# Attention with mixed heads and an expert layer: eight score tiles in a ring inside a larger tile, and a late store in two parts

## The chip, the core and the metric
The kernel runs on one core of one Trainium2 chip. The metric is the time of one execution on the device in microseconds (us). Before the change the median of three runs is 1441.89 us.

## The reference
```python
scores = scale * np.matmul(q, k.transpose(0, 1, 3, 2))       # 8 batches, 12 heads, 448 x 448
scores = np.einsum('bhij,hg->bgij', scores, w_pre)           # heads mixed
scores = scores - np.max(scores, axis=-1, keepdims=True)
attn = np.exp(scores)
attn = attn / (np.sum(attn, axis=-1, keepdims=True) + 1e-09)
attn = np.einsum('bhij,hg->bgij', attn, w_post)              # heads mixed again
x = np.matmul(attn, v)                                       # to (8*448, 12*64)
out = (((x @ w1) * (x @ w2)) @ w3) @ w_out                   # the expert layer
```
All of it is float32; the expert weights are 64-bit words in HBM that the kernel turns into floats itself.

## The kernel before
The main loop in `run` goes over steps n. A block is 10 rows of scores (queries) with all 12 heads; there are 45 blocks in a batch, and one step stands for one block. Work goes in pairs m of blocks, two steps for each.

Scores pass through HBM to change their layout. `qk` computes 128 rows of scores for two heads into two PSUM banks (psq, L174), ACT copies them into an SBUF tile `st` (L179, L180), and one DMA stores the tile to `raw_d` (L188; L185 for the last 64 rows of a pair). `fetch` reads a pair of blocks back (L202) with heads and rows on the partitions, two DMAs into a tile `r` of which there are two. `mix` multiplies it with the first head matrix (psm, L220), `largest` takes row maxima on DVE (L227), `exp` runs on ACT (L235), `scale` makes the second head matrix divided by the sums (DVE L244, L245, POOL L247), `post` multiplies with it (pso, L260), and `put` copies the result to a tile `mt` (ACT L274). `mt` holds 150 columns of queries; there are two buffers of it. `av` multiplies an `mt` block with v (psa, L301).

Beside that, `converting` turns the words of w3, w_out and later w1 and w2 into floats: a DMA into a tile cs (L103, five of them), a square on ACT (cm, L110), four instructions on DVE (cx, L121 to L124), then a split into two parts (ACT L129, POOL L130). `folding` multiplies w3 with w_out (psf, L360).

All order is written out by hand: each engine runs its instructions as the loop emits them, and nothing is rescheduled. SP issues every DMA in that order, and a DMA waits on SP for the landing of what it reads and for the semaphore that it takes; eight semaphores (DMAHW0 to DMAHW7) are taken in turn.

Score tiles come from two pools with two tiles each: `kp`, and for odd pairs of heads of batch 0 `qp`, which is closed at step 16. Before the loop, the first 128 rows of batch 0 are computed for all 12 heads into one tile `sz`. It takes the first of the two `mt` buffers, of which it uses 12 x 448 of 7200 columns. Its rows 0 to 47 are stored at once, in six DMAs; rows 48 to 127 in one DMA, `held`, behind the first two fetches and one DMA of weight words. Block pair 2 (rows 40 to 59) reads from both. The second `mt` block is first written by the `put` of step 17. In the loop, steps 0 to 11 compute the other rows of batch 0, steps 12 to 14 its last 64 rows, and from step 11 on the scores of batch 1 are added, about three units in four steps.

Of the kernel before, what the change touches and what calls it, by code (L numbers as in the profile page):

```python
# [6 lines left out]
F32 = mybir.dt.float32  # L7
# [8 lines left out]
B, H, S, D = 8, 12, 448, 64  # L16
DM, FF = 768, 1024
HP = H // 2
# [3 lines left out]
QT, NJ = 128, 4  # L22
# [5 lines left out]
PP = 64  # L28
JB = S // PP
SETS = NB * B // 2  # L30
FIRST = 48
# [2 lines left out]
LATE = 2 * NB + GB + 2  # L34
PAIRS = ((0, 0), (0, 1), (1, 0))
N_UP, NS = 20, 50
DEEP = 5
ONE = 2


# [10 lines left out]
class Kernel:  # L51
# [44 lines left out]
    def ask_words(self, depth):  # L96

        while len(self.asked) < depth and self.sources:
            src, n = self.sources.pop(0), self.n_words
            s = self.cs.tile([128, CW, 2], I32, tag="s", name=f"cs{n}", bufs=DEEP)  # L100
            a, k = src.shape[1], src.shape[2] // 2
# [30 lines left out]
    def converting(self, jobs, late=False):  # L132
# [5 lines left out]
        for n in range(len(jobs) + 1):  # L138
            self.ask_words(min(3 + self.n_made // 2, DEEP))
            yield  # L140
# [19 lines left out]
    def parts(self, b, p, c):  # L160
# [2 lines left out]
            return [(self.kqs[0, p], j * PP + S * (j > 1), QT) for p, j in pairs]  # L163
        return [(self.kqs[b, p], j * PP, S) for p, j in pairs]

    def qk(self, b, p, c, banks):


        nc = self.nc
        ps = [self.bank(i, f"psq{b}_{p}_{c}_{s}")[:, :S] for s, i in enumerate(banks)]  # L170
        for z, (t, q, k) in enumerate(self.parts(b, p, c)):
            for s in range(2):
                rows = slice(s * D, (s + 1) * D)
                nc.tensor.matmul(ps[s][z * PP:(z + 1) * PP], t[rows, q:q + PP], t[rows, k:k + S], start=True, stop=True)  # L174
        if b == c == 0:
            st = self.sz[:, 2 * p:2 * p + 2]
        else:
            st = (self.qp if b == 0 and p % 2 else self.kp).tile([128, 2, S], F32, tag="st", name=f"st{b}_{p}_{c}", bufs=2)
        nc.scalar.copy(st[:, 0], ps[0])  # L179
        (nc.vector.tensor_copy if b == c == 0 else nc.scalar.copy)(st[:, 1], ps[1])  # L180
        raw = self.raw_d[b]
        if c == 3:
            def store():
                for z in range(2):
                    nc.sync.dma_start(raw[3 * QT:, 2 * (p + z) - 2:2 * (p + z)], st[z * PP:(z + 1) * PP])  # L185
            return store
        n = QT if b or c else FIRST
        return lambda: nc.sync.dma_start(raw[c * QT:c * QT + n, 2 * p:2 * p + 2], st[:n])  # L188
# [280 lines left out]
    def sums(self, w, f, k):  # L469
# [8 lines left out]
        def split(m, i):  # L478
            s = self.cs.tile([128, CW, 2], I32, tag="s", name=f"s{w}_{f}_{m}", bufs=DEEP)
            s = s.rearrange("p n b -> p (n b)").bitcast(F32)  # L480
            dst, x = self.s_d[w][m][f].rearrange("p (t n) -> p t n", t=2), y[:, i]
            hi, lo = s[:, :n], s[:, n:2 * n] if w < 2 else x
            nc.scalar.copy(hi.bitcast(F32R), x)
            nc.gpsimd.tensor_tensor(lo.bitcast(F32R), x, hi, op=ALU.subtract)
            if w < 2:
                self.later.append(lambda: nc.sync.dma_start(self.s_d[w][m][f], s))
            else:
                self.later.append(lambda: nc.sync.dma_start(dst[:, 0], hi))
                self.later.append(lambda: nc.sync.dma_start(dst[:, 1], lo))
# [251 lines left out]
    def run(self):  # L741
        nc, tc = self.nc, self.tc
# [29 lines left out]
            self.kqs[0, p] = self.qp.tile([128, 2 * S], F32, tag="kq", name=f"kqz{p}")  # L772
            nc.sync.dma_start(self.kqs[0, p][:, :QT + S], self.kq0[p][:, :QT + S])
        self.sz = self.mp.tile([QT, NJ, H, GB * IB], F32, tag="mt", name="sz")
        self.sz = self.sz.rearrange("p j g i -> p (j g i)")[:, :H * S].rearrange("p (h j) -> p h j", h=H)
        w = self.kp.tile([128, 2, S], F32, tag="st", name="wpre_s", bufs=2)[:, 0, :PP]
        self.wsc = cp.tile([128, PP], F32, name="wsc")
        nc.sync.dma_start(w, self.wpre)
# [2 lines left out]
        for p in self.pso:  # L781
            for s in range(2):
                at = (2 * NJ - 2 + s) * HK
# [11 lines left out]
        held = []  # L795
# [6 lines left out]
        next(fold_pieces)  # L802
        for f in held:
            f()
        held = lambda: nc.sync.dma_start(self.raw_d[0][FIRST:QT], self.sz[FIRST:])

# [67 lines left out]
        others(1)  # L876
        for m in range(LF // 2):
            self.fetch(m)
        next(fold_pieces)
        next(fold_pieces)  # L880
        held()
        next(fold_pieces)
        next(fold_pieces)
        self.mix(0)
# [4 lines left out]
        for n in range(N + 6):  # L889
# [45 lines left out]
            p, pieces = self.n_made - 1 if fold_pieces else 2 * KF + 3 * KF, None  # L935
            if avs.get(n):
                pass
            elif fold_pieces:
                f = (self.n_made - 1 - 2 * KF) // 3
# [112 lines left out]
```

## Time and profile before
| | us |
|---|---|
| median of three runs | 1441.89 |
| lowest, highest run | 1441.69, 1447.07 |
| the profiled execution | 1437.83 |
| its span, first to last instruction | 1436.1 |

| engine | busy us | share |
|---|---|---|
| PE (matmuls) | 1382.4 | 96% |
| ACT | 832.4 | 58% |
| DVE | 741.1 | 52% |
| POOL | 620.3 | 43% |

The profile is of one execution on the chip. Each engine's instructions have a start and a length there, and idle time before an instruction is put down to what ended it. A DMA shows twice: its issue on SP, and its landing, when the last of its 16 engines has told its semaphore. [...] The DMA share is the mean busy share of the 16 DMA engines; it can pass 1, since packets of one engine overlap.

### The profile page before, as it was taken

Reading aid. Unit: us, or ns where it says so; the run is one execution under the profiler, and the core shown is the slowest. Engines: PE = TensorE matmul, PEld = TensorE weight load, DVE = VectorE, ACT = ScalarE, POOL = GpSimd, SP = SyncE. Lnnn points to the kernel's source line nnn. Section 1 sums busy time; section 2 is a strip of 40 time slices with the busy share of each in tenths; the row PEclk is TensorE's granted clock in tenths of the full one; section 3 lists DMA queues with packets and bytes.
Section 4 is the critical chain, followed back from the end, with each engine's and each line's share of the span. In section 5 each row is a group of like instructions: output and inputs, shape, how many; then the busy total and the mean of one; then the engine's idle time right before and its main releaser. Section 6 shows DMA issues by size and latency. Waiting matters only on the chain.

```text
span 1436.1 us, 45775 instructions
## 1 busy us (share of the span) xinstructions
PE 1382.4 (96%) x18684; PEld 1055.2 (73%) x18684; DVE 741.1 (52%) x1497; ACT 832.4 (58%) x1952; POOL 620.3 (43%) x754
## 2 busy tenths in 40 slices
PE   5889999999999999999999999999999999999998
PEld 2457786776677667776777777777777777899988
DVE  6867566767544544432444436334444446345563
ACT  4867666777766666665656556556555445422231
POOL 2433233434433544532345336334335446446693
PEclk7989999999999999999999999999999999999999
DMA  8998789999999999999989979799879757698775
GB/s 294 366 326 279 236 270 322 320 312 317 324 286 348 355 356 330 362 346 349 287 275 290 320 259 280 249 323 354 288 229 281 241 177 223 195 337 270 231 232 171
DMA packets 203761, 416.87 MB, mean 290 GB/s; under 512 B 20528, under 2 KB 120112, under 8 KB 203472
## 3 DMA queue, kind: packets, MB, share of 16 engines
q1 hardware_dynamic: 203552, 413.94, 87.6%
q8 instruction: 149, 2.44, 0.7%
q14 instruction: 60, 0.49, 0.1%
HBM read 279.77 MB, written 134.09 MB: 288 GB/s over the span
## 4 chain that ended last, share of the span: by engine, by line
PE 82%; DMA 8%; DVE 4%; ACT 2%; issue 1%; POOL 1%; SPq 0%; DVEq 0%; POOLq 0%; ACTq 0%
PE e L702 21%; PE psa L301 11%; PE pso L260 10%; PE psm L220 9%; PE psq L174 7%; PE eg L522 5%; PE psf L360 4%; PE eo L553 4%; PE e2o L702 4%; PE e1o L702 4%; PE e3o L702 4%; DMA wu<-w_d 3%; DMA r<-raw_d 2%; DMA raw_d<-st 2%; ACT e L235 1%
## 5 line engine op out<-in xcount | busy, mean ns | idle before, releaser
L247 POOL TENSOR_SCALAR w<-wpo,ri 128x60 f32<-128x60 f32 x360 | 180.7, 518 | 485.1 <-DVE ri L245 465.3
L227 DVE TENSOR_REDUCE mn<-psm 128x1 f32<-128x448 f32 x360 | 207.7, 618 | 321.6 <-PE psm L220 321.3
L274 ACT COPY mt<-pso 128x480 f32<-128x480 f32 x352 | 197.9, 621 | 185.8 <-PE pso L260 185.6
L702 PE MATMUL e<-eh,wu 128*128 128x448 f32 x1008 | 296.8, 371 | 6.4 <-DVE c L656 3.2
L235 ACT ACTIVATE e<-psm,mn 128x448 f32<-128x448 f32 x360 | 226.8, 643 | 7.9 <-DVE mn L227 7.9
L702 PEld LDWEIGHTS e<-eh,wu 128*128 128x128 f32 x1008 | 187.5, 188 | 52.2 <-issue 26.8
L260 PEld LDWEIGHTS pso<-w,e 60*64 60x64 f32 x10080 | 175.2, 135 | 51.0 <-issue 42.5
L220 PE MATMUL psm<-r,wsc 60*64 60x448 f32 (+1 forms) x1440 | 191.2, 550 | 19.1 <-DVE cx L124 8.3
L260 PE MATMUL pso<-w,e 60*64 60x60 f32 x10080 | 199.1, 224 | 0.4 <-ACT mt L274 0.3
L702 PE MATMUL e<-el,wu 128*128 128x448 f32 x504 | 186.9, 371 | 0.0
L301 PE MATMUL psa<-mt,v 128*64 128x150 f32 (+1 forms) x2304 | 156.9, 292 | 4.1 <-ACT st L179 4.1
L301 PEld LDWEIGHTS psa<-mt,v 128*64 128x64 f32 x2304 | 143.6, 137 | 20.1 <-ACT st L179 6.7
L174 PE MATMUL psq<-kq 64*64 64x448 f32 x1176 | 154.6, 542 | 2.4 <-ACT st L179 2.4
L656 DVE TENSOR_TENSOR c<-c,e 128x448 f32<-128x448 f32 x168 | 101.7, 618 | 87.7 <-PE e L702 82.9
L179 ACT COPY st<-psq 128x448 f32<-128x448 f32 x162 | 86.4, 533 | 73.7 <-ACT mt L274 34.1
L522 PE MATMUL eg<-xh,wu 128*128 128x448 f32 x384 | 119.2, 381 | 6.3 <-DMA wu<-w_d 6.3
L641 POOL TENSOR_TENSOR el<-x,eh 128x448 fp32r<-128x448 f32 x90 | 103.7, 1170 | 32.8 <-ACT eh L640 29.9
L702 PEld LDWEIGHTS e<-el,wu 128*128 128x128 f32 x504 | 94.6, 188 | 22.5 <-issue 14.1
L174 PEld LDWEIGHTS psq<-kq 64*64 64x64 f32 x1176 | 60.8, 135 | 56.4 <-issue 28.8
L522 PEld LDWEIGHTS eg<-xh,wu 128*128 128x128 f32 x384 | 71.9, 190 | 38.7 <-issue 24.0
L244 DVE TENSOR_SCALAR sa<-sm 128x2 f32<-128x2 f32 x180 | 34.9, 194 | 113.6 <-ACT e L235 113.1
L180 ACT COPY st<-psq 128x448 f32<-128x448 f32 x162 | 87.6, 541 | 0.0
(99 smaller groups left out, 2010.1 us busy)
## 6 DMA issues: line engine op xcount, KB each, us to landing
r<-raw_d SPq DMA_DIRECT2D x344, 210.0 KB, 5.1
raw_d<-st SPq DMA_DIRECT2D x138, 448.0 KB, 6.1
wu<-w_d SPq DMA_DIRECT2D x104, 384.0 KB, 6.7
wu<-s_d SPq DMA_DIRECT2D x96, 384.0 KB, 4.8
wu<-w_d SPq DMA_DIRECT2D x51, 512.0 KB, 5.5
kq<-kq SPq DMA_DIRECT2D x42, 448.0 KB, 7.0
wu<-s_d SPq DMA_DIRECT2D x36, 512.0 KB, 4.9
x<-x_d SPq DMA_DIRECT2D x72, 224.0 KB, 5.7
```

The lines of the kernel that those rows point to most:

```text
L174: nc.tensor.matmul(ps[s][z * PP:(z + 1) * PP], t[rows, q:q + PP], t[rows, k:k + S], start=True, stop=True)
L220: nc.tensor.matmul(ps[s][c * PP:(c + 1) * PP, :S], self.wsc[k], r[k, c], start=True, stop=True)
L227: self.nc.vector.tensor_reduce(mn[:, s:s + 1], self.psm[m][s][:, :S], axis=AX.X, op=ALU.min)
L235: nc.scalar.activation(e, p[:, :S], AF.Exp, bias=mn[:, s:s + 1], scale=-1.0, accum_out=sm[:, s:s + 1])
L247: nc.gpsimd.tensor_scalar_mul(w2[:, s], self.wpo, ri[:, s:s + 1])
L260: nc.tensor.matmul(self.pso[c][z * PP:(z + 1) * PP, at:at + HK], e[k, j * PP:(j + 1) * PP], w2s[k, s], start=True, stop=True)
L274: self.nc.scalar.copy(dst.rearrange("p j g (s i) -> p j s g i", s=2), src)
L301: nc.tensor.matmul(self.psa[rows, g % 3, :W], v[:, j, rows], mt[:, j, 2 * g + s, :W], start=(j == 0), stop=(j == NJ - 1))
L522: nc.tensor.matmul(p, u[:, k % (K1 // 2), x], xs[y][:, k], start=(k == 0 and t == 0), stop=(k == K1 - 1 and t == 2))
L641: nc.gpsimd.tensor_tensor(lo, x, hi.bitcast(F32), op=ALU.subtract)
L656: nc.vector.tensor_tensor(a[out], a[to[0]], p, op=ALU.add)
L702: nc.tensor.matmul(p, w[:, k, x], ops[m, k][y], start=(k == 0 and t == 0), stop=(k == nk - 1 and t == 2))
```

## The change
From the first score tile of step 0 up to step 14, `next_st` hands out eighths of the buffer in which `sz` lies: eight places of 2 x 448 columns in turn, the first two behind the end of `sz`, then its six, then again from the start. From step 15 on tiles come from `kp`, two of them. The late store of rows 48 to 127 becomes two: 16 rows ahead of the next DMA of weight words, and 64 rows where the whole store stood.

```diff
-DEEP = 5
+DEEP, RING = 5, 14
...
+    def next_st(self, name):
+        if self.step > RING:
+            return self.kp.tile([128, 2, S], F32, tag="st", name=name, bufs=2)
+        self.n_st += 1
+        at = (self.n_st + HP - 1) % 8 * 2 * S
+        return self.sz_all[:, at:at + 2 * S].rearrange("p (h j) -> p h j", h=2)
...
-            st = (self.qp if b == 0 and p % 2 else self.kp).tile([128, 2, S], F32, tag="st", name=f"st{b}_{p}_{c}", bufs=2)
+            st = self.next_st(f"st{b}_{p}_{c}")
...
-        self.sz = self.sz.rearrange("p j g i -> p (j g i)")[:, :H * S].rearrange("p (h j) -> p h j", h=H)
+        self.sz_all, self.n_st = self.sz.rearrange("p j g i -> p (j g i)"), 0
+        self.sz = self.sz_all[:, :H * S].rearrange("p (h j) -> p h j", h=H)
...
-        held = lambda: nc.sync.dma_start(self.raw_d[0][FIRST:QT], self.sz[FIRST:])
+        rest = [lambda k=k: nc.sync.dma_start(self.raw_d[0][k], self.sz[k]) for k in (slice(FIRST, PP), slice(PP, QT))]
...
         for m in range(LF // 2):
             self.fetch(m)
+        rest[0]()
         next(fold_pieces)
         next(fold_pieces)
-        held()
+        rest[1]()
```

On SP, ahead of the loop, before (r are the fetches of pairs 0 and 1, cs the weight words, sz the tile of the first scores; the brackets name the semaphores that a DMA waits for):
```order
20 L202 DMA r_219<-raw_d 60x2x448 [waits DMAHW5_49,DMAHW4_49,DMAHW7_49,DMAHW3_49,DMAHW0_49]
21 L202 DMA r_219<-raw_d 60x2x448
22 L202 DMA r_222<-raw_d 60x2x448
23 L202 DMA r_222<-raw_d 60x2x448 [waits DMAHW6_49]
24 L103 DMA cs_225<-wo 128x768
25 L805 DMA raw_d<-sz 80x5376
26 L103 DMA cs_238<-wo 128x768 [waits DMAHW1_49]
```
The same place in the changed kernel:
```order
20 L209 DMA r_219<-raw_d 60x2x448 [waits DMAHW5_49,DMAHW4_49,DMAHW7_49,DMAHW3_49,DMAHW0_49]
21 L209 DMA r_219<-raw_d 60x2x448
22 L209 DMA r_222<-raw_d 60x2x448
23 L209 DMA r_222<-raw_d 60x2x448 [waits DMAHW6_49]
24 L813 DMA raw_d<-sz 16x5376
25 L103 DMA cs_226<-wo 128x768
26 L813 DMA raw_d<-sz 64x5376 [waits DMAHW1_49]
```
The 80 rows at place 25 are now 16 rows at place 24 and 64 at place 26; each DMA behind them stands one place later and takes the next semaphore.

On ACT, steps 15 to 17, before (st_1_0, st_1_1 and st_1_2 are score tiles of batch 1, mt_1 is the second mt block):
```order
112 L179 COPY st_1_0_1078<-psq_1_0_0_1072 128x448 [waits DMAHW3_49,PE_49]
...
118 L179 COPY st_1_1_1114<-psq_1_1_0_1108 128x448 [waits DMAHW1_49,PE_49]
...
122 L274 COPY mt_0_414<-pso_141 128x4x2x12x5 [waits PE_49]
123 L274 COPY mt_1_1165<-pso_142 128x4x2x12x5 [waits PE_49]
124 L179 COPY st_1_2_1180<-psq_1_2_0_1174 128x448 [waits DMAHW1_49,PE_49]
125 L180 COPY st_1_2_1180<-psq_1_2_1_1175 128x448 [waits PE_49]
```
The same rows in the changed kernel:
```order
112 L186 COPY st_1_0_1061<-psq_1_0_0_1055 128x448 [waits PE_49]
...
118 L186 COPY st_1_1_1097<-psq_1_1_0_1091 128x448 [waits PE_49]
...
122 L281 COPY mt_0_412<-pso_141 128x4x2x12x5 [waits PE_49]
123 L281 COPY mt_1_1148<-pso_142 128x4x2x12x5 [waits DMAHW4_49,DMAHW3_49,DMAHW5_49,DMAHW2_49,DMAHW6_49,DMAHW1_49,DMAHW7_49,DMAHW0_49,PE_49]
124 L186 COPY st_1_2_1163<-psq_1_2_0_1157 128x448 [waits DMAHW2_49,PE_49]
125 L187 COPY st_1_2_1163<-psq_1_2_1_1158 128x448 [waits PE_49]
```
No instruction moved on ACT. The copies of steps 15 and 16 wait for no DMA any more, the first write of the second mt block waits for eight, and the copy of step 17 waits for the store of step 15's tile, as before.

## Rows read from the trace of the kernel before
**Rows 1.** The page, part 1: busy us, share of the span, instructions.
```profile
PE 1382.4 (96%) x18684; PEld 1055.2 (73%) x18684; DVE 741.1 (52%) x1497; ACT 832.4 (58%) x1952; POOL 620.3 (43%) x754
```
**Rows 2.** Stretches (us): length, busy per engine, granted clock, DMA share, GB/s.
```profile
24.00:28.00 4.00, 3.78 (x16) 1.32 (x16) 1.36 (x4) 2.04 (x7) 1.79 (x3) 0.50 0.89 325
28.00:32.00 4.00, 3.47 (x15) 1.46 (x13) 3.72 (x7) 3.08 (x8) 1.00 (x1) 0.50 0.99 266
32.00:62.00 30.00, 25.55 (x410) 13.70 (x413) 28.23 (x57) 26.31 (x64) 13.25 (x18) 0.91 1.02 365
62.00:96.00 34.00, 25.42 (x294) 13.38 (x286) 23.54 (x44) 21.67 (x52) 11.53 (x14) 0.80 1.03 367
...
110.00:300.00 190.00, 185.80 (x2781) 139.91 (x2770) 130.03 (x272) 133.92 (x322) 64.74 (x91) 1.00 0.90 292
```
**Rows 3.** Timeline, ACT: start, us, instruction, idle before it and what ended that.
```profile
64.47 0.53 ACT L179 COPY st<-psq 128x448 f32<-128x448 f32 x1 [0.62 <-DMA raw_d<-st]
...
70.45 0.53 ACT L179 COPY st<-psq 128x448 f32<-128x448 f32 x1 [2.90 <-PE psm L220]
...
74.11 0.53 ACT L179 COPY st<-psq 128x448 f32<-128x448 f32 x1 [2.69 <-DMA raw_d<-st]
...
78.42 0.53 ACT L179 COPY st<-psq 128x448 f32<-128x448 f32 x1 [1.48 <-DMA raw_d<-st]
...
95.72 0.53 ACT L179 COPY st<-psq 128x448 f32<-128x448 f32 x1 [4.05 <-DMA raw_d<-st]
```
**Rows 4.** DMA from 62 to 96 us: issues, KB each, median us to landing.
```profile
DMA packets 6527, 12.48 MB, mean 367 GB/s; under 512 B 602, under 2 KB 4068, under 8 KB 6524
...
raw_d<-st SPq DMA_DIRECT2D x8, 448.0 KB, 7.6
r<-raw_d SPq DMA_DIRECT2D x9, 210.0 KB, 7.4
```
**Rows 5.** Timeline, SP: start and length of DMA issues.
```profile
26.99 0.81 SPq L202 DMA_DIRECT2D r<-raw_d  x2
...
77.41 1.40 SPq L202 DMA_DIRECT2D r<-raw_d  x2
...
84.20 1.10 SPq L185 DMA_DIRECT2D raw_d<-st  x2
```
**Rows 6.** Timeline, the other engines.
```profile
23.00 0.56 ACT L110 ACTIVATE cm<-cs 128x384 f32<-128x384 f32 x1 [4.47 <-DMA cs<-wo]
...
28.10 0.36 DVE L121 TENSOR_SCALAR cx<-cs 128x384 int32<-128x384 int32 x1 [2.60 <-DMA cs<-wo]
...
32.42 0.53 ACT L179 COPY st<-psq 128x448 f32<-128x448 f32 x1
...
88.22 0.59 PE L220 MATMUL psm<-r,wsc 60*64 60x448 f32 x1
...
90.58 3.59 PE L360 MATMUL psf<-fo,fw 128*128 128x384 f32 x19
...
96.31 3.28 PE L301 MATMUL psa<-mt,v 128*64 128x150 f32 x48 [2.13 <-ACT st L179]
```
**Rows 7.** Chain that ended last: start, us, what (a DMA from issue to landing).
```profile
17.18 0.42 SPq L805
...
17.65 10.36 DMA cs<-wo
...
87.56 8.09 DMA raw_d<-st
```
**Rows 8.** Waits of SP, 10 to 110 us: in total, times, longest.
```profile
SPq L202 <- DMA raw_d<-sz: 5.5, 3, 4.5
```
**Rows 9.** Three shorter stretches, columns as in rows 2.
```profile
92.12:95.54 3.42, 2.05 (x12) 1.73 (x10) 2.72 (x6) 0.00 (x0) 0.18 (x1) 1.00 1.02 379
518.79:522.20 3.41, 0.63 (x4) 0.34 (x3) 1.90 (x5) 3.04 (x8) 0.05 (x1) 1.00 1.02 324
522.20:525.61 3.41, 3.41 (x10) 2.87 (x11) 1.50 (x3) 0.00 (x0) 2.71 (x3) 0.50 1.03 408
```

## The prediction
> **What bounds the kernel now.** I read the page first: TensorE (PE) is busy for 96% of the span, ACT and DVE for little more than half [rows 1]. Such a share hides stages, so the second view was the table by stretches [rows 2]. From 110 us on PE is busy 185.80 of 190 us: what comes before counts only by when that stage begins. The change touches steps 0 to 17, which lie before 97 us. Two other limits rule there. From 32 to 62 us VectorE (DVE) is busy 28.23 of 30 us; it turns the 64-bit weight words into floats. From 62 to 96 us PE is busy 25.42 of 34, DVE 23.54, ACT 21.67, and the DMA share is 1.03 at 367 GB/s.
>
> The third view, the timeline of that stretch, shows what the engines wait for [rows 3]: ACT's copies of scores into an st tile stand still for 0.62, 2.90, 2.69, 1.48 and 4.05 us. Four are put down to the store that last read the tile. The second names PE's L220; but that copy needs only its own two score banks and its tile, so it was a store there too. A reader may take these 11.74 us for a lack of tiles. The fourth view says what is behind them [rows 4]: 12.48 MB in 35 transfers (the counts of that answer's nine rows), 357 KB each. SP's instructions show eight DMA semaphores in rotation, so eight transfers can be under way, and eight of 357 KB at 367 GB/s take 7.8 us. A 448 KB store takes 7.6 us from issue to landing and an r fetch 7.4. So the queue is full, and a landing is set by the bytes ahead of it, not by when its data was ready.
>
> **The change, part by part.** Matmuls, conversions, copies and their order on PE, ACT, DVE and POOL stay. SP gets one DMA more; bytes and the order of the others are the same.
>
> *The ring.* Up to step 14 a copy waits for the store eight tiles back, where it waited for one two to four back. The copies of rows 3 start 3.7 us apart or more; at half of that, eight tiles are still 15 us, twice what a store needs. So the waits of 0.62, 2.90, 2.69 and 1.48 us go, 7.69 in all. What is late next? What PE then asks for is itself a landing from the full queue. The r fetches issued from 77.41 on, the second within 1.4 us [rows 5], land at 7.4 us each by about 85.8; their mix ran at 88.22 [rows 6], so it comes 2.4 us sooner and no more. Then come step 17's scores. From step 15 the two old st tiles serve again: the copy of step 17 takes the tile of step 15, whose store was issued at 87.56 and landed 8.09 us later, at 95.65 [rows 7]. It stands behind the same bytes as before, so its landing does not move. That copy started at 95.72 [rows 3], and behind it PE's attention product (psa) at 96.31 [rows 6]; from there PE is the limit. The 7.69 us are given back as a longer wait before this copy. Value taken: 0; bounds -7.69 and 0.
>
> *The new wait.* The second block of mt lies in the ring's buffer, so its first write waits for all the ring's stores, on all eight semaphores. It stands on ACT just ahead of the step-17 copy; queued behind it are that copy, a cast, a square and the next exponentials, and PE's psa waits for the copy. The last ring stores were issued from 84.20 to 85.30 [rows 5]; even at 7.6 us they land by 92.9, 2.7 us under the copy's own release at 95.65. Cost 0; were that cover gone, whatever they land later than the copy's tile.
>
> *The late store.* Before, 80 rows (1680 KB) went in one transfer at 17.18 [rows 7]. The fetch of the third pair of blocks reads rows 48 to 59 out of it and was issued only at 26.99 [rows 5]; SP, which issues in order, stood 4.5 us for the landing [rows 8]. Now 16 rows go first and the fetch waits for them alone, so SP gets on some 4 us sooner. But the queue was hardly empty meanwhile: its share was 0.89 from 24 to 28 us and 0.99 from 28 to 32, at 325 and 266 GB/s [rows 2]. At the 365 GB/s of the next stretch these eight us would have given 4 x 40/365 + 4 x 99/365 = 1.5 us; if the rates come from the small rows of r and kqz, nothing. Against it stands one more issue on SP, 0.42 us like the old one's [rows 7]. Bounds -1.5 and +0.4; I take -0.5, nearest to the idle share (4 x 0.11 = 0.44). It would carry through to the landing at 95.65, since the queue stays full in between.
>
> The first words of the output weights now come behind 16 rows (336 KB), 0.9 us at 367 GB/s. ACT had stood 4.47 us for them until 23.00 [rows 6], so this moves to 23.9. The words behind the store land where they did, at 28.01 [rows 7], and DVE had idled 2.60 us before those [rows 6]: cost 0, and up to 0.9 if that slack is used up.
>
> The words behind the whole store landed 1.0 us after SP was released by it (28.01 against 26.99), 384 KB at about the queue's rate: transfers follow one another closely. [...]
>
> *PE's clock.* PE's last work ahead of psa, 19 psf matmuls at 90.58 to 94.17 [rows 6], would end about 2.4 us sooner, and PE would stand over 4 us for psa, where it stood 2.1. [...] At 0.50 from 95.8 to 99.0, 1.6 us of PE's work is lost, where PE is the limit. Bounds 0 (clock kept) and 3.3 (low for 6.6 us); I take 1.6.
>
> **The sum:** ring 0, new wait 0, late store -0.5, first words 0, clock +1.6: +1.1 us. On the profiled execution's 1437.83 us (span 1436.1 and 1.7 around it) that is 1438.9. The median of the runs was 1441.89, 4.06 above that execution, so the forecast is 1443.0.
>
> **Rivals.**
> *The tiles were the limit: faster.* If stores landed sooner once ACT runs ahead, the 7.69 us would be PE's: 1441.9 - 7.7 = 1434.2. For it: ACT's idle time names the stores. Against it: a share of 1.03 over 34 us leaves nothing to send sooner. It decides at one place: the store issued at 87.56 must land by about 88. [...]
> *The clock falls and comes back late: slower.* PE stands before psa, and the clock is at 0.50 for two stretches like that of rows 9, from 95.8 to 102.4: +3.3. If besides the queue gains nothing and the first words cost their 0.9, it is +4.2: 1446.1. [...] For it: from 24 to 32 us the clock stayed at 0.50 though PE was busy 7.25 of 8 us [rows 2]. Against it: after 522.20, with PE busy throughout, it was back after 3.41 us [rows 9].
> *The ring doesn't do what it says.* Its third copy writes into the old tile, so it waits for both parts of the late store. The store was through by 26.99, that copy ran at 32.42 [rows 6], 5.4 us later; were the second part that much later, all of the ring would stand behind it. Price 0 as the rows are: 1441.9.
>
> **How the numbers follow.** Forecast 0.70 (own range 1440.4, which is -1.5 with the clock kept, to 1444.8, which is +1.6 with late words and the issue), tiles 0.13, clock slower 0.12, ring idle 0.05. Half a per cent, 7.2 us, is about what a measurement of this kernel can tell from no change. Faster means under 1434.7: half of the first rival, 0.06. Slower means over 1449.1, past every priced case: 0.03. The same has the rest, 0.91. The range runs from 1436.5 (two thirds of the tiles' gain) to 1446.5.
>
> **What would show it.** Right: ACT's waits for stores between 64 and 85 us gone; its wait before the step-17 copy, or before the mt write ahead of it, grown to 8 us or more; psa within 1.5 us of 96.31; the DMA share still near 1.03 up to 96 us; the third pair's fetch issued at about 22.5; a stretch at 0.50 close behind 95.5. Wrong: psa several us sooner, or a DMA share clearly under 1 before it.

## The result and the profile after

The changed kernel has a median of 1446.51 us (1442.57 to 1451.02, 15 runs); the kernel before, timed beside it, 1441.75 (1439.82 to 1447.07, 15 runs). The ratio is 1.0030, 95% interval 1.0016 to 1.0043: 2.3 to 6.2 us slower. That is under half a per cent, but no longer zero. 1443.0 was forecast; the median lies at the upper edge of the forecast's range (1446.5) and outside the narrower one that it gave itself (1440.4 to 1444.8).

The page, part 1, for the changed kernel (busy us, share, instructions) answers to [rows 1]; its span is 1448.0 us. PE's busy time rose by 3.3 us, while the two profiled spans differ by 11.9, so most of the difference is waiting:
```profile
PE 1385.7 (96%) x18684; PEld 1057.3 (73%) x18684; DVE 742.4 (51%) x1497; ACT 832.0 (57%) x1952; POOL 619.7 (43%) x754
```
Stretches of the changed kernel, with the columns of [rows 2]:
```profile
24.00:28.00 4.00, 3.46 (x16) 1.12 (x16) 1.65 (x5) 2.37 (x7) 1.79 (x3) 0.66 0.86 190
28.00:32.00 4.00, 1.25 (x6) 0.68 (x3) 0.18 (x1) 0.19 (x1) 0.00 (x0) 0.91 0.87 263
32.00:62.00 30.00, 23.90 (x353) 12.04 (x356) 28.30 (x54) 25.90 (x62) 12.93 (x17) 0.89 1.04 357
62.00:96.00 34.00, 24.29 (x358) 13.78 (x349) 27.50 (x53) 24.16 (x59) 12.85 (x16) 0.95 1.03 367
...
110.00:300.00 190.00, 186.73 (x2813) 140.73 (x2810) 127.84 (x265) 132.01 (x317) 62.64 (x88) 0.99 0.89 289
```
From 62 us on these rows read as forecast (DMA share 1.03 up to 96 us). What was not forecast stands in the first two: from 24 to 28 us the queue is as busy as before (0.86 against 0.89) but moves 190 GB/s where it moved 325, and from 28 to 32 us DVE works 0.18 us where it worked 3.72. Its next weight words were not there.

The timeline of the changed kernel, ACT and DVE at the weight words (answers to [rows 6]), then ACT and PE before psa (answers to [rows 3, 6]):
```profile
23.32 0.56 ACT L110 ACTIVATE cm<-cs 128x384 f32<-128x384 f32 x1 [4.07 <-DMA cs<-wo]
...
31.81 0.56 ACT L110 ACTIVATE cm<-cs 128x384 f32<-128x384 f32 x1 [5.44 <-DMA cs<-wo]
31.82 0.36 DVE L121 TENSOR_SCALAR cx<-cs 128x384 int32<-128x384 int32 x1 [6.00 <-DMA cs<-wo]
...
93.50 0.61 ACT L281 COPY mt<-pso 128x480 f32<-128x480 f32 x1 [4.54 <-DMA cs<-w3t]
97.13 0.53 ACT L186 COPY st<-psq 128x448 f32<-128x448 f32 x1 [3.01 <-DMA raw_d<-st]
```
```profile
97.71 1.52 PE L308 MATMUL psa<-mt,v 128*64 128x150 f32 x10 [4.01 <-ACT st L186]
```
DVE's row stood at 28.10 with 2.60 us of idle time before it; now at 31.82 with 6.00. None of ACT's score copies between 64 and 85 us waits for a store any more. In their place ACT stands 4.54 us before the first write of the second mt block and 3.01 before the copy of step 17, and psa starts at 97.71 instead of 96.31. The profile names weight words for the first of these; the write waits for eight semaphores, and the ring's last store, issued at 87.7, landed about then too (its stores took 5.7 to 6.2 us here).

SP in the changed kernel (start, us, DMAs), the late store's parts and what is behind them (answers to [rows 5]):
```profile
17.25 0.41 SPq L813 DMA_DIRECT2D raw_d<-sz  x1
17.70 0.42 SPq L103 DMA_DIRECT2D cs<-wo  x1
18.16 2.28 SPq L813 DMA_DIRECT2D raw_d<-sz  x1
20.49 2.73 SPq L103 DMA_DIRECT2D cs<-wo  x2
23.26 2.49 SPq L881 DMA_DIRECT2D kqz<-kq  x1
25.87 2.15 SPq L209 DMA_DIRECT2D r<-raw_d  x2
```
The same place before, behind the whole store (issued at 17.18 in 0.42 us):
```profile
17.65 2.82 SPq L103 DMA_DIRECT2D cs<-wo  x2
20.51 1.96 SPq L873 DMA_DIRECT2D kqz<-kq  x1
```
SP was to reach the third pair's fetch at about 22.5. It does so at 25.87: it no longer waits for the store's landing, but these issues alone fill the time. Before, two of them took 2.29 and 1.96 us and the others about 0.4; now four take 1.6 to 2.5. The second words are issued at 20.49 instead of 17.65 and take 11.24 us to land instead of 10.36.

The clock at psa (two stretches of the changed kernel; the answer to [rows 9]; the third number from the end is the granted clock, 1.00 at full speed):
```profile
96.99:100.40 3.41, 2.69 (x22) 2.56 (x24) 1.27 (x3) 2.94 (x8) 1.00 (x1) 0.50 1.00 349
100.40:103.81 3.41, 3.41 (x94) 2.83 (x94) 0.69 (x2) 1.00 (x2) 0.83 (x2) 1.00 0.85 298
```
This is the forecast stretch: PE stood 4.01 us, the stretch from 96.99 on ran at a granted clock of 0.50, and psa's 48 products took from 97.7 to 102.0 where they took from 96.3 to 99.3: 1.3 us.

So at 110 us the same PE instruction starts 2.7 us later than before. The two profiled executions end 12 us apart, but they lie 3.9 under and 3.3 over the medians above; the medians (4.8 apart) don't bear out what the two gain and lose on each other behind 300 us. The readings below therefore use the stage up to 110 us and, for the time, the medians.

### The profile page after: what moved, and what is told of

Read it like the earlier page. It is cut to its first block, busy times and chain, and to the rows that moved or that the text cites. A ratio compares the mean times of both kernels' runs of the same rounds, so it can differ in the third digit from the quotient of the medians.

```text
span 1448.0 us, 45770 instructions
## 1 busy us (share of the span) xinstructions
PE 1385.7 (96%) x18684; PEld 1057.3 (73%) x18684; DVE 742.4 (51%) x1497; ACT 832.0 (57%) x1952; POOL 619.7 (43%) x754
## 4 chain that ended last, share of the span: by engine, by line
PE 80%; DMA 10%; DVE 5%; ACT 3%; issue 1%; SPq 1%; POOL 0%; DVEq 0%; POOLq 0%; ACTq 0%
PE e L709 21%; PE psa L308 10%; PE pso L267 10%; PE psm L227 9%; PE psq L181 7%; PE eg L529 6%; PE psf L367 4%; PE e2o L709 4%; PE e3o L709 4%; PE e1o L709 4%; PE eo L560 3%; DMA wu<-w_d 2%; DMA r<-raw_d 2%; DMA raw_d<-st 2%; ACT e L242 1%
## 5 line engine op out<-in xcount | busy, mean ns | idle before, releaser
L227 PE MATMUL psm<-r,wsc 60*64 60x448 f32 (+1 forms) x1440 | 194.9, 556 | 24.5 <-DMA r<-raw_d 12.4
L181 PE MATMUL psq<-kq 64*64 64x448 f32 x1176 | 158.4, 547 | 0.6 <-ACT st L186 0.6
L186 ACT COPY st<-psq 128x448 f32<-128x448 f32 x144 | 76.8, 533 | 72.9 <-ACT mt L281 35.3
L315 ACT COPY xd<-psa 128x450 f32<-128x450 f32 (+1 forms) x36 | 19.2, 533 | 116.0 <-PE psa L308 116.0
```

The lines of the kernel that those rows point to most:

```text
L227: nc.tensor.matmul(ps[s][c * PP:(c + 1) * PP, :S], self.wsc[k], r[k, c], start=True, stop=True)
```

## The experiments

A DMA's packets stand in the trace one by one. The late store makes 80 of 21,504 bytes, one for each row, whether it goes whole or in parts (split by heads, 160 of half the size). 80 are five for each of the 16 DMA engines over which the page takes its share, in the mean; no trace shows which engine takes which row. "Packet" below is their mean duration. "At 110" is how much later than in the kernel before (minus: sooner) the same PE instruction starts there, in the one profiled execution.

| | packet us | psa starts | at 110 | ratio to before, 95% |
|---|---|---|---|---|
| before | 0.87 | 96.31 | 0 | 1 |
| changed kernel | 1.38 | 97.71 | +2.7 | 1.0030 (1.0016 to 1.0043) |
| ring, whole store | 0.85 | 94.63 | -1.7 | 0.9999 (0.9983 to 1.0015) |
| split alone | 1.48 | 96.41 | +0.1 | 1.0013 (0.9997 to 1.0030) |
| ring, 32 + 48 rows | 1.29 | 97.0 | +2.4 | 1.0021 (1.0004 to 1.0037) |
| ring, whole store first | 1.05 | 95.0 | -1.2 | 1.0017 (0.9999 to 1.0035) |
| ring, split by heads | 0.52 (half size) | 96.1 | -0.2 | 1.0015 (1.0002 to 1.0028) |
| ring, 64 then 16 rows | 1.30 | 97.6 | +3.0 | 1.0019 (1.0005 to 1.0034) |
| ring, five strided parts | 0.93 | 96.2 | +1.6 | 1.0010 (0.9989 to 1.0031) |
| ring, five adjacent parts | 1.51 | 99.6 | +5.0 | 1.0030 (1.0012 to 1.0048) |
| ring, third tile | | 92.24 | -4.1 | 0.9973 (0.9960 to 0.9985) |
| ring, fewer v bytes | | 93.37 | -1.3 | 0.9994 (0.9976 to 1.0012) |
| third tile, no ring | | 92.37 | -3.9 | 0.9996 (0.9977 to 1.0014) |
| ring to step 13, third tile | | 90.47 | -5.8 | 0.9971 (0.9955 to 0.9987) |

Two things have to be kept in mind with this table. The clock fell at psa in five more kernels (32 + 48 rows, 64 then 16 rows, both five-part kernels, fewer v bytes): psa's 48 products took 4.9 to 5.0 us there instead of 3.28, and their column "at 110" holds these 1.7 us. PE had stood 2.58 to 4.41 us for psa where the clock fell, and at most 2.56 where it did not, so the length of that wait alone does not tell the two apart. And the times lie above the stage in most rows: the whole store first is 1.2 us ahead at 110 with a ratio of 1.0017, the split by heads 0.2 ahead with 1.0015. What comes of it behind 110 us is open.

**Which half of the change costs the time.** First the ring alone:
```diff
-        rest = [lambda k=k: nc.sync.dma_start(self.raw_d[0][k], self.sz[k]) for k in (slice(FIRST, PP), slice(PP, QT))]
+        held = lambda: nc.sync.dma_start(self.raw_d[0][FIRST:QT], self.sz[FIRST:])
...
-        rest[0]()
...
-        rest[1]()
+        held()
```


> The ring alone; the late store stays one transfer at its old place. Theory (the split slows the transfer): the 80 row packets are back at 0.87 us each (1.38 us in the changed kernel), the second words land at about 28.0 again, DVE's idle time before them is 2.6 and not 6.0 us, psa starts 2.7 us sooner than in the changed kernel. What is left is the ring: 0 from the full queue and a stretch at 0.50 before psa, +1.6 (0 to 3.3). Against the kernel before: -0.5 to +2. Rival (the ring itself costs the time, through the clock and the wait of the second mt block): about +4.8, as the whole change.

The packets are back at 0.85 us, the second words at 28.60, and nothing is left of the slowdown. The stretch at 0.50 that was expected at psa lay earlier, from 86.2 to 89.6 us, where PE's work was not what psa waited for. Stretches of the ring with the whole store, then its ACT and PE before psa:
```profile
24.00:28.00 4.00, 3.90 (x17) 1.41 (x17) 1.24 (x4) 1.93 (x6) 1.79 (x3) 0.50 0.90 327
62.00:96.00 34.00, 23.94 (x320) 14.91 (x314) 25.22 (x49) 24.16 (x57) 12.37 (x16) 0.95 1.03 374
```
```profile
90.75 0.62 ACT L281 COPY mt<-pso 128x480 f32<-128x480 f32 x1 [5.50 <-DMA r<-raw_d]
94.04 0.53 ACT L186 COPY st<-psq 128x448 f32<-128x448 f32 x1 [2.68 <-DMA raw_d<-st]
```
```profile
94.63 3.28 PE L308 MATMUL psa<-mt,v 128*64 128x150 f32 x48 [2.47 <-ACT st L186]
```
psa starts 1.7 us sooner than in the one profile of before, and runs at full clock; the times show no gain. In the changed kernel the split costs 3.1 us at psa (97.71 - 94.63) and the clock 1.3 behind it. The split alone is the other half (the two-part store put into the kernel before):

> The late store in 16 + 64 rows, with the score tiles of the kernel before. Theory (the split slows the transfer): second words land at about 31.7, ACT's waits for stores between 64 and 85 us are all there as before, PE reaches psa 3 to 4 us later than before; +2.5 to +4 us against the kernel before. Rival (the ring costs it): within 0.5 us of the kernel before.

Its stretch from 24 to 28 us and its psa:
```profile
24.00:28.00 4.00, 3.42 (x16) 1.31 (x16) 1.68 (x5) 2.41 (x7) 1.79 (x3) 0.50 0.86 172
```
```profile
96.41 2.77 PE L301 MATMUL psa<-mt,v 128*64 128x150 f32 x40 [1.07 <-ACT st L179]
```
The packets slow down as expected (1.48 us; 172 GB/s), and at 35 us PE is 2.9 us late. But at 97 us it is 0.1 late: without the ring the waits for tiles take the loss up (the copy of step 17 waits 2.40 us instead of 4.05). PE was to reach psa 3 to 4 us late, which it did not; 2.5 us or more was expected of the time and 1.9 measured (-0.4 to 4.3). So the packets are clear and the time is undecided.

**Sizes and places.** In the changed kernel, the parts `slice(FIRST, FIRST + 32)` and `slice(FIRST + 32, QT)`; then a single part, `slice(FIRST, QT)`, at the first one's place.

> As the changed kernel, but the parts are 32 and 48 rows, two and three rows for each DMA engine in place of one and four. Theory, first form (rows four apart collide: 64 rows over 16 engines): the packets of the 48 rows take about 0.8 to 0.9 us, the second words land 1.5 to 3.5 us sooner than in the changed kernel, and the time is 1.5 to 3 us lower. Second form (any split at these places slows it, whatever the sizes): packets at 1.3 us or more in the mean and the same time as the changed kernel.

> With the ring; the late store is one transfer of 80 rows, but at the place of the first part, ahead of the weight words. Theory (the split, not the place, slows the packets): mean packet about 0.87 us; the first words behind it come 3.5 to 4.5 us later than before (1680 KB at 367 to 430 GB/s), so ACT stands longer for them, and the time is 0 to +4 us against the kernel before. Rival (the earlier place slows the packets, since they then share the queue with the fetches of the first pairs): mean packet over 1.2 us and +4 us or more.

With 32 and 48 rows half of the packets take 0.80 us, most others 1.5 to 2.4 and the longest 3.31; the second words come 0.7 us sooner and the time does not change. That is the second form, and the idea that only rows four apart collide is out. The whole store at the early place is between its two cases, at 1.05: the earlier place, beside the fetches, costs something. Its words came late (ACT stood 9.39 us for them, and PE was 5.4 us late at 25 us), and yet psa started at 95.0: in this kernel the lateness was made up again.

```diff
-        rest = [lambda k=k: nc.sync.dma_start(self.raw_d[0][k], self.sz[k]) for k in (slice(FIRST, PP), slice(PP, QT))]
+        rest = [lambda k=k: nc.sync.dma_start(self.raw_d[0][FIRST:QT, k], self.sz[FIRST:, k]) for k in (slice(0, HP), slice(HP, H))]
```


> With the ring and with both parts at the places of the change, but each part is all 80 rows of six heads: packets of 10.5 KB, five rows for each DMA engine as in the whole store. The fetch now waits for both parts. Theory (which rows the engines read at the same time decides the packets): packets near 0.40 to 0.45 us, half of the whole store's 0.85, second words landed by 28 to 29, psa within 1 us of the ring with the whole store (94.6). Rival (two big stores in the queue with words between them slow each other, whatever the rows): packets over 0.6 us, second words at 30.5 or later, psa 1.5 to 3 us later than 94.6.

Here two parts of 80 rows: most packets (116 of 160) take 0.40 us, half of 0.80. So two parts as such don't double a packet's time. But the mean is 0.52, above the 0.40 to 0.45 expected, and psa is 1.5 us later than with the whole store, where 1 us was the theory's limit and 1.5 to 3 the rival's. What stands beside that: its first words came at 26.75 (22.88 there), and the third pair's fetch, which waits for both parts, was issued at 28.73 (27.06). For the next run both parts stand at the whole store's place, 64 rows ahead of 16:

> With the ring; both parts at the place of the whole store, 64 rows first and then 16. Theory (the rows decide): from the second row of each engine on, the 64-row part's packets go in step at about 1.67 us, mean of all over 1.2 us, and 28 us is reached with 0.5 to 0.9 MB less than with the whole store. Rival (the place ahead of the first words, and the words in between, slow it): packets near 0.85 us and the second words at about 28.3, as with the whole store.

The first twenty or so packets take 0.80 us, many later ones 1.67, those of the 16 rows mostly 2 to 2.9. That is the theory, at the old place.

**Which rows travel together.** The cleanest pair: five parts of 16 rows each at the old place, which differ only in the rows.
```diff
+        parts = [slice(FIRST + k, QT, 5) for k in range(5)]
+        held = lambda: [nc.sync.dma_start(self.raw_d[0][k], self.sz[k]) for k in parts]
```
The other has `slice(k, k + 16) for k in range(FIRST, QT, 16)`.

> [...] Theory (the rows that the engines read at one time decide how long a packet takes): most packets at 0.80 us though there are five parts, mean under 1.1 us, and the MB moved by 28 us within 0.3 of the whole store's 7.97. Rival (the number of parts decides): packets in step at 1.6 us or more, as in the kernel with 64 and 16 rows, or longer.

> As the run with five strided parts, but each part is 16 neighbouring rows. Theory (the rows decide): packets of a part go in step at 1.6 us or more, mean at least 0.4 us over that of the strided parts, and 0.5 MB or more behind it by 28 us. Rival (the number of parts decides, or nothing but their bytes): the same as the strided parts within 0.15 us a packet.

Packets take 0.93 and 1.51 us in the mean, those of an adjacent part up to 3.09 (29 of the 80 took 0.80). By 28 us 7.59 and 7.03 MB had passed; the strided parts missed the 0.3 MB within which they were expected of the whole store's 7.97. At psa five strided parts cost 1.6 us over the whole store, and the choice of rows 3.3 us more. The stretch from 20 to 28 us, in this order: before, changed kernel, ring with the whole store, five strided parts, five adjacent parts.
```profile
20.00:28.00 8.00, 6.04 (x29) 1.63 (x22) 3.44 (x8) 3.04 (x8) 1.79 (x3) 0.50 0.98 366
```
```profile
20.00:28.00 8.00, 5.83 (x31) 1.75 (x23) 3.44 (x8) 3.05 (x8) 1.84 (x4) 0.71 0.93 254
```
```profile
20.00:28.00 8.00, 6.35 (x32) 1.91 (x24) 3.44 (x8) 3.05 (x8) 1.79 (x3) 0.50 0.95 361
```
```profile
20.00:28.00 8.00, 6.26 (x32) 2.16 (x28) 3.44 (x8) 3.05 (x8) 2.05 (x4) 0.71 0.99 328
```
```profile
20.00:28.00 8.00, 5.17 (x30) 1.53 (x22) 3.44 (x8) 3.04 (x8) 1.79 (x3) 0.92 1.07 247
```
What counts are the last two numbers of each: the DMA share says 0.93 to 1.07, the bytes 247 to 366 GB/s. It is shown that the rows that travel together set most of the loss of rate (328 GB/s strided, 247 adjacent); the five parts as such, or their later place on SP, the smaller rest (361 to 328). The reason is not shown. In the kernel before, 66 of the whole store's 80 packets took 0.80 us, and the slow ones stand near multiples of that: 1.67 us is 2.1 times 0.80, and 3.09, the longest, is 3.9 times. What makes a packet slow beside its neighbours no run shows. The rows of a part decide which partitions are read together and also which addresses in HBM are written together, and no run moves the one apart from the other.

**What psa waits for.** To the ring with the whole store, a free tile for step 17 (ahead of `if self.step > RING`):
```diff
+        if self.step == RING + 1:
+            return self.qp.tile([128, 2, S], F32, tag="st", name=name, bufs=1)
```


> The ring with the whole store, and step 15's tile comes from the pool of the odd pairs, so that step 17's copy finds a free tile. Theory A (that tile's store was the last wait before psa): the copy goes at about 91.3 behind the mt write and psa starts at about 92, 2.6 us sooner than with the ring and the whole store (94.6), 4.3 sooner than before; time 1.5 to 3 us lower than with the ring and the whole store if nothing comes late behind it. Theory B (the full queue sets the pace, as the prediction had it): psa sooner, but the fetches behind it land at 97.7 as they did, PE stands there instead, and from 110 us on nothing is gained over the ring with the whole store.

Its psa:
```profile
92.24 3.28 PE L310 MATMUL psa<-mt,v 128*64 128x150 f32 x48 [1.00 <-ACT st L188]
```
Theory A: 4.1 us are gained over before and kept at 110 (2.4 over the ring with the whole store), and of the ratios so far 0.9973 is the first with its whole interval under 1. Then the same idea without ring or split (`or self.step == GB` in the old choice of the pool):

> No ring and no split: the kernel before, and only step 15's tile comes from the pool of the odd pairs. Theory A (the one wait that counted in the kernel before was step 17's copy on step 15's tile): psa starts 2 to 4 us sooner than 96.3 and the time is 1.5 to 3.5 us lower than before. Theory B (the ring is needed too, since the waits of 64 to 85 us come later as a late psf and late scores): psa no more than 1.5 us sooner, time within 1.5 us of before.

```profile
92.37 3.28 PE L301 MATMUL psa<-mt,v 128*64 128x150 f32 x48
```
In the profile it gains as much, and the times say 0.9996 (0.9977 to 1.0014). Theory A by the trace, B by the time; the intervals of the two kernels overlap, and this stays open. Next, step 14's tile goes there too (`DEEP, RING = 5, 13`, two tiles in that pool):

> The ring with the whole store up to step 13 only; the tiles of steps 14 and 15 come from the pool of the odd pairs, so the first write of the second mt block no longer waits for the stores of step 14 (landed at 90.9 with a third tile). Theory (the mt write on the ring's last stores is what psa waits for then): the mt write goes at 88 to 89, psa starts right behind PE's psf, 0.5 to 1.2 us sooner than 92.2; time 0 to 1 us under the ring with a third tile. Rival (PE's order ahead of psa is the bound already): psa within 0.3 us of 92.2.

The first write of the second mt block goes at 86.21 instead of 91.15, and psa starts right behind psf, 1.8 us sooner; more than expected. PE of this kernel:
```profile
86.95 3.58 PE L369 MATMUL psf<-fo,fw 128*128 128x384 f32 x19
90.47 3.28 PE L310 MATMUL psa<-mt,v 128*64 128x150 f32 x48
```
No idle time is left before psa. Its ratio is 0.9971 (0.9955 to 0.9987), not to be told apart from the third tile's, but under the kernel before, and so under the changed one (1.0016 at its lowest). By psa and the stage up to 110 us it is the best version.

**Is the queue the limit?** In the ring with the whole store, `t[:, :k]` with k = 1 for batch 0 in `load_v`, and its only block for all four in psa:

> The ring with the whole store; of batch 0's v only a quarter is loaded and used (that part of the computation is changed), so six transfers between 47 and 75 us carry 64 KB each instead of 256: 1.18 MB less, 3.2 us of the queue at 367 GB/s. Theory (the queue of transfers sets the stages up to 96 us): psa starts 2 to 3.2 us sooner than 94.6, at 91.4 to 92.6. Rival (the engines' own work or the tiles set it): psa within 0.7 us of 94.6.

In between: psa starts 1.3 us sooner, not 2 to 3.2. Between 62 and 70 us the share was 1.03, as full as ever, at 348 GB/s (390 in the ring with the whole store). The chain of this kernel at step 15's store (start, us; the answer to [rows 7]):
```profile
86.21 6.50 DMA raw_d<-st
...
93.37 3.68 PE psa L309 x29
```
With 1.18 MB less the store is issued 1.4 us sooner than with all of v (86.21 against 87.60). The queue sets part of the pace, not all of it. At 110 us nothing of it is left (-1.3 against -1.7), since the clock fell at psa:
```profile
93.37 4.96 PE L309 MATMUL psa<-mt,v 128*64 128x150 f32 x48 [3.05 <-ACT st L186]
```

## Why the prediction was right, and where it was not

*The ring: 0 forecast, -1.7 measured.* The mechanism held. The ring with the whole store ran 7.5 us ahead (PE at 80 us) and had given it back when step 15's store was issued: 87.60 against 87.56 [rows 7]. What failed is "its landing does not move". It moved from 95.65 to 93.97, since the store took 6.37 us instead of 8.09. In the nine other kernels whose chain shows this wait it took 6.07 to 6.70, with and without the ring: the term rested on one landing of one execution, the slowest of them all, and the -1.7 may be no more than that. The rival of tiles that were the limit had 7.69; that much was never there, but by the traces 4 us were, at one tile that the prediction had named and taken for covered by the queue: with a free tile the copy of step 17 went right behind the mt write.

*The new wait: 0 forecast.* In the changed kernel the mt write waited 4.54 us, but the copy behind it ended later by its own tile. A cover of 2.7 us was forecast, and 3.01 us is what the copy still waited. Together the two waits are 7.55 us; the sign of 8 or more in one of them did not come. With a third tile the cover was gone, and there the wait cost 1.8 us.

*The late store: -0.5 forecast (-1.5 to +0.4); it cost 3.1 us at psa.* This is the step that failed. "Bytes and the order of the others are the same" was true, and "the words behind the store land where they did, at 28.01" did not follow: they landed at 31.73. By 28 us 7.13 MB had passed instead of 8.04; 0.91 MB are 2.5 us at 367 GB/s, of the 3.7 that the words were late. The rest is not separated: their issue came 2.84 us later, behind an issue of 2.28 us for the 64 rows, and with five strided parts, whose packets were hardly slower, the words were still about 1 us later than with the whole store. The gain forecast from SP's earlier fetch was not there either: 25.87 instead of 22.5. The bounds came from the queue's share and rate, as if a byte cost the same in each transfer.

*The first words: 0 forecast.* They came at 23.32 against 23.00, a third of the 0.9 us allowed.

*PE's clock: +1.6 forecast, +1.3 measured,* at the place and for the length of one stretch (3.41 us at 0.50). The 1.6 was the author's estimate: half of one stretch at 0.50, after a wait of PE like one in [rows 9]. How long a wait brings such a stretch no run shows. With the ring and the whole store PE stood 2.47 us before psa, and the clock was kept.

The sum was +1.1; the stage gives -1.7 + 3.1 + 1.3 = +2.7, and the times +2.3 to +6.2. Two mis-sized terms of opposite sign kept it close, and that is luck. The slower rival, 1446.1, came nearest to the median, but not by its own mechanism: the clock was back after one stretch, and the first words cost a third of their price. The rival of an idle ring did not come: the ring's third copy ran at 36.16 without waiting, 7.9 us behind the last packet of the late store. Between +2.7 and the middle of the times, +4.3, 1.6 us are open. They would go if the -1.7 belongs to the one slow landing: against the ring with the whole store, split and clock make 4.4 us at psa, and the two ratios are 4.5 us apart. That fits, and no run shows it.

## What to carry to other kernels

Look at which rows of a tile a transfer moves at one time before cutting it: here many packets of 64 adjacent rows took 1.67 us and those of 16 adjacent rows up to 3.09, where most of the whole store's took 0.80, while strided rows stayed at 0.93 in the mean and half of each row in all 80 at 0.52, though no cut made the kernel faster than the whole store did. Judge a queue by GB/s beside its busy share: here the share stayed near 1 (0.98 before, 0.93 in the changed kernel, from 20 to 28 us) while the GB/s fell by a third (366 to 254), and the mean packet took 1.38 us instead of 0.87. When an engine's waits are all put down to one resource, ask which of them is the last before the stage that counts; here a ring of eight tiles moved psa by 1.7 us at most, where one tile at the end moved it by 2.4 to 3.9 (the time followed with the ring; without it that is open). And take the duration of one landing for what it is: one sample.

## What was not expected of the hardware

The packets of one DMA, all of 21,504 bytes, took 0.80 us (66 of the 80 of the whole store in the kernel before), about 1.67 (21 of the changed kernel's 80 between 1.60 and 1.70) or up to 3.09 (16 adjacent rows), by which rows went together. SP's issues around the late store, 0.4 us as a rule, took up to 2.5 us each in the changed kernel, and 5.02 for two behind one another in the split by heads.
